# ScalarE instead of VectorE for one of two PSUM copies in the transposes of a retention + FFN kernel

## Chip, cores and metric

The kernel runs on one core of one Trainium2 chip. The metric is the device time of one execution in microseconds, lower is better. Four executions of the kernel before took 983.06, 985.38, 981.36 and 984.71 us, a median of 983.89 us.

The engines are called by the names that the profile uses: PE (matrix products, with PEld for its weight loads), DVE (VectorE), ACT (ScalarE), POOL (GpSimd) and SP (SyncE, which here only issues DMAs).

## What is computed

Attention with decay ("retention", without softmax) for 8 batches, 8 heads, 576 tokens and head dimension 64. Its output is laid out as 4608 tokens of 512 features, and goes through an FFN with a squared ReLU (512 to 2048 to 512). All of it is float32.

```python
scores = scale * np.matmul(q, k.transpose(0, 1, 3, 2))
gamma = 1.0 - 2.0 ** (-5.0 - np.arange(H, dtype=np.float32))
rel = pos[:, None] - pos[None, :]
Dmat = np.where(rel >= 0, gamma[:, None, None] ** rel[None, :, :], 0.0)
attn_out = np.matmul(scores * Dmat[None, :, :, :], v)
x = np.ascontiguousarray(attn_out.transpose(0, 2, 1, 3)).reshape(B * S, H * D)
h = np.maximum(x @ w_in, 0.0)
out = h * h @ w_out
```

## The kernel before

**Chunks.** The tokens of each batch are cut into chunks of 128, the last of a batch having 64: five chunks for each batch, 40 in all, numbered through. Chunks 4 and 9 are therefore short ones. A state per head (`u_ps` in PSUM, `u_sb` in SBUF) carries what earlier chunks of the batch leave to later ones. The finished tokens go to `xT` in SBUF, and blocks of 512 of them to the FFN.

**Order.** The program is written out in one order by hand, and each engine runs its own instructions in that order. The main loop (L753) runs over the chunks. For chunk numbers from 5 on, its body puts these calls one after the other:

- `retain_a(i - 1)` (L476): half of chunk i-1's own products into `x_ps`, and growth of the state, which ACT copies (L474);
- `turn(i)` (L414) while i is under `N_TURN` = 11, the function of the change;
- `ffn(i - 1, 0)` (L706): some steps of the FFN, enough to keep a pace;
- `retain_b(i - 1)` (L491): products of the earlier state with q (PE L500), and then L503, a tiny ACT copy of 128x2 that reads `x_ps` and writes into a state buffer;
- `scores(i)` (L428): k times q into PSUM (PE L443, 32 matmuls of 64x64, or 16 for a short chunk), masked by DVE (L451) and written over k's place;
- `retain_c(i - 1)` (L505): the other half of the chunk's own products (PE L465). The first of them waits for L503. Then ACT copies the result to `xT` (L522) and the state (L474);
- `ffn(i - 1, 1)`, and the loads of q, k and v for a later chunk.

Chunks 0 to 4 (`N_EARLY` = 4) have an order of their own at L754 to L795; chunk 4 is turned there, ahead of `retain_b(3)`.

**Turning q and k.** The products need q and k with the head dimension on the partitions. For chunks 0 to 10 PE transposes them through the identity matrix (L422): first k, then q, 64x64 at a time, into one PSUM tile `t_ps` of two banks. k and q of the first 64 tokens lie in the one bank, those of the second 64 in the other. Two copies bring them to the SBUF tile `qk`: k by ACT (L425), q by DVE (L426). From chunk 11 on, `flip` does without PE and PSUM: DVE transposes 32x32 blocks (L396) and ACT moves each to its place (L411, 416 copies of 32x256).

`t_ps` has one buffer (L107), and for chunks from 4 on `scores` takes the same one (L436). So PE can only start chunk i's scores when q and k of that chunk have been copied out, and can only turn the next chunk when DVE has masked the scores.

**What else these engines do in this stretch.** While chunks 4 to 10 are turned, FFN block 0 runs (`first_in`, L576: PE L586, ReLU by ACT at L591, squares by DVE at L594). Its weights come in as 64-bit floats and are turned to float32 in the meantime, 16 pieces of w_in, each by five DVE instructions (L210, L214, L222, L225, L228) with two ACT instructions (L218, L219) between the second and the third. POOL scales q (L376) and v (L453) when they have landed. SP issues all loads and stores of this stretch, in program order. From chunk 10 on, FFN blocks 1 and later run in a form with seven products (`ffn_in`, L607: PE L622, ACT L632 and L638, DVE L629 to L648). After the last chunk, a second long phase multiplies by w_out (PE L928).

Of the kernel before, what the change touches and what calls it, by code (L numbers as in the profile page):

```python
# [40 lines left out]
def kernel(  # L41
# [33 lines left out]
    nc = tc.nc  # L75
# [54 lines left out]
    N_EARLY = TOK // C  # L130
# [227 lines left out]
    def rows(half, n=64):  # L358
        return slice(64 * half, 64 * half + n)
# [24 lines left out]
    def new_qk(i):  # L384
        t = work3.tile([128, 2, HP, C], F32, tag="qk", name="qk")
        st[i]["qT"], st[i]["kT"] = t[:, 0, :, :], t[:, 1, :, :]
        return t
# [26 lines left out]
    def turn(i):  # L414

        cs = chunks[i][3]
        n_h = cs // CH
        p = ps_t.tile([128, 2, 512], F32, tag="t", name="t_ps").rearrange("p h (j d t) -> p h j d t", j=2, d=HP)
        for j in (1, 0):
            for hp in range(HP):  # L420
                for h in range(n_h):
                    nc.tensor.transpose(p[:, h, j, hp, :], loaded[i][j][rows(h), 2 * hp:2 * hp + 2, :],  # L422
                                        ident[rows(h), rows(h)])
        to = new_qk(i)[:, :, :, :cs].rearrange("p j d (h t) -> p j d h t", h=n_h)
        nc.scalar.copy(to[:, 1].rearrange("p d h t -> p h d t"), p[:, :n_h, 1, :, :])  # L425
        nc.vector.tensor_copy(to[:, 0].rearrange("p d h t -> p h d t"), p[:, :n_h, 0, :, :])  # L426

    def scores(i):  # L428

# [320 lines left out]
    warm(6, True)  # L750
    scale_q(0, nc.vector)
    turn(0)
    for i in range(N_CH + 1):  # L753
        if i <= N_EARLY:  # L754
# [5 lines left out]
            if i >= 1:  # L760
                retain_a(i - 1)
                if i < 3:
                    warm(4, False)
                elif i == N_EARLY:
                    turn(i)
                else:
                    convert(1)
                    first_in(1, (0,))
                    convert(5)
                retain_b(i - 1)  # L770
                if i < 3:
                    warm(4, False)
                retain_c(i - 1)
# [17 lines left out]
            if i < N_EARLY:  # L791
                if i < 2:
                    warm(6, False)
                if i + 1 < N_EARLY:
                    turn(i + 1)  # L795
# [283 lines left out]
```

## Time and profile before

The profiled execution took 983.06 us, of which 981.3 us are the span from the first to the last instruction. The table gives the busy time of each engine, in microseconds, in stretches of that span.

| stretch (us) | length | PE | PEld | DVE | ACT | POOL |
|---|---|---|---|---|---|---|
| 0 to 36 (start, chunks 0 to 3) | 36 | 28.57 | 24.87 | 19.33 | 13.64 | 13.04 |
| 36 to 102 (chunks 4 to 9 turned, FFN block 0) | 66 | 64.48 | 36.10 | 57.14 | 31.56 | 12.80 |
| 102 to 128 (chunk 10 turned, flips begin) | 26 | 24.54 | 19.09 | 20.82 | 13.84 | 5.59 |
| 140 to 155 | 15 | 14.81 | 12.34 | 14.83 | 9.01 | 3.97 |
| 155 to 400 | 245 | 237.01 | 201.19 | 206.79 | 154.98 | 58.17 |
| 400 to 981 (end of the first phase, w_out) | 581 | 574.68 | 548.49 | 453.50 | 107.04 | 30.09 |

PE's granted clock was 1.00 in all of these stretches but the first (0.95).

A busy share says how long an engine had something in hand, and not that its work set the pace. The table is only a first look; what an engine waited for, and for how long, is read from the views of waits and from the timeline.

### The profile page before, as it was taken

What the parts mean: (1) busy time and instruction counts of PE and PEld (TensorE: products, weight loads), DVE (VectorE), ACT (ScalarE), POOL (GpSimd) and SP (SyncE); (2) the same over time, 40 slices, a digit from 0 to 9 for tenths busy, and PEclk for the clock granted to TensorE, in tenths of its full rate; (3) what the DMA queues carried; (4) which work ended last, traced back from release to release, by engine and by line L of the source; (5) the groups of instructions that cost most, each with busy time, mean ns of one, the idle gap of its engine ahead of it and who ended that gap; (6) DMA issues with size and microseconds to landing.
All of it is one profiled execution on the core that took longest, in us unless ns stands there. A gap on an engine that the chain in (4) does not pass through costs nothing. (4 is left out here: it accounts for less than half of the span.)

```text
span 981.3 us, 24018 instructions
## 1 busy us (share of the span) xinstructions
PE 956.1 (97%) x10108; PEld 852.4 (87%) x10108; DVE 783.5 (80%) x1447; ACT 341.4 (35%) x848; POOL 127.4 (13%) x121
## 2 busy tenths in 40 slices
PE   7999999999999989989999999999999999999998
PEld 6745787888778878878888889999999999999998
DVE  3889799978887988788756588878888787887876
ACT  2554484674755855846541010000000000000000
POOL 3211223312122221213201000000000000000000
PEclk9999999999999999999999999999999999999999
DMA  9975656685586767656635966645353454534241
GB/s 201 246 222 150 179 154 161 213 274 147 153 240 197 208 173 235 172 144 140 236 135 232 361 246 247 226 161 184 108 204 116 175 186 174 204 116 172 87 172 43
DMA packets 172011, 181.43 MB, mean 185 GB/s; under 512 B 118144, under 2 KB 132480, under 8 KB 165248
## 3 DMA queue, kind: packets, MB, share of 16 engines
q1 hardware_dynamic: 169792, 179.38, 57.8%
q8 instruction: 79, 1.29, 0.5%
q10 hardware_dynamic: 2112, 0.52, 0.3%
q14 instruction: 28, 0.23, 0.1%
HBM read 109.36 MB, written 70.52 MB: 183 GB/s over the span
## 5 line engine op out<-in xcount | busy, mean ns | idle before, releaser
L622 PE MATMUL h_b<-room,w 128*128 128x256 f32 x768 | 186.6, 386 | 6.7 <-DVE room L641 3.7
L411 ACT COPY qk<-flip 32x256 f32<-32x256 f32 x416 | 167.4, 402 | 16.4 <-DVE flip L396 10.8
L622 PEld LDWEIGHTS h_b<-room,w 128*128 128x128 f32 x768 | 144.0, 191 | 29.0 <-DVE room L641 4.9
L928 PE MATMUL o_b<-w,room 128*128 128x128 f32 x1168 | 144.4, 275 | 0.2 <-DVE room L880 0.2
L928 PEld LDWEIGHTS o_b<-w,room 128*128 128x128 f32 x1168 | 137.2, 192 | 0.4 <-DVE room L880 0.4
L928 PE MATMUL o_c<-w,room 128*128 128x128 f32 x1008 | 123.0, 275 | 0.0
L622 PE MATMUL h_a<-room,w 128*128 128x256 f32 x512 | 122.5, 382 | 0.0
L622 PE MATMUL h_c<-room,w 128*128 128x256 f32 x512 | 122.1, 381 | 0.0
L928 PEld LDWEIGHTS o_c<-w,room 128*128 128x128 f32 x1008 | 117.7, 192 | 0.0
L942 ACT COPY r<-o_a 128x128 f32<-128x128 f32 x53 | 14.1, 266 | 271.7 <-PE o_a L928 236.1
L622 PEld LDWEIGHTS h_a<-room,w 128*128 128x128 f32 x512 | 96.0, 190 | 13.9 <-issue 0.5
L622 PEld LDWEIGHTS h_c<-room,w 128*128 128x128 f32 x512 | 96.4, 190 | 13.4
L928 PE MATMUL o_a<-w,a 128*128 128x128 f32 x688 | 85.6, 275 | 0.0
L928 PEld LDWEIGHTS o_a<-w,a 128*128 128x128 f32 x688 | 81.2, 192 | 0.1
L639 POOL TENSOR_TENSOR room<-room 128x512 f32<-128x512 f32 x32 | 34.8, 1088 | 346.2 <-ACT room L638 291.6
L629 DVE SCALAR_TENSOR_TENSOR room<-room 128x512 f32<-128x512 f32 x96 | 71.7, 747 | 3.3
L586 PE MATMUL h_ps<-room,w 128*128 128x512 f32 (+1 forms) x152 | 59.7, 540 | 1.4 <-DVE w L228 0.7
L465 PEld LDWEIGHTS x_ps<-qk,v_ld 64*64 64x64 f32 x1152 | 40.8, 138 | 19.5 <-issue 12.8
L641 DVE TENSOR_TENSOR room<-h_b,room 128x512 f32<-128x512 f32 x32 | 22.0, 687 | 44.6 <-PE h_b L622 44.6
L376 POOL TENSOR_TENSOR q_ld<-q_ld,dv 128x512 f32<-128x512 f32 (+1 forms) x39 | 45.0, 1153 | 92.8 <-DMA q_ld<-in_q_dram 72.0
L465 PE MATMUL x_ps<-qk,v_ld 64*64 64x64 f32 x1152 | 50.3, 227 | 6.4 <-ACT u_sb L503 6.0
L453 POOL TENSOR_TENSOR v_ld<-v_ld,dv 128x512 f32<-128x512 f32 (+1 forms) x40 | 48.5, 1214 | 12.9 <-DMA v_ld<-in_v_dram 12.9
(104 smaller groups left out, 1344.5 us busy)
## 6 DMA issues: line engine op xcount, KB each, us to landing
g_dram<-room SPq DMA_DIRECT2D x32, 1280.0 KB, 5.7
a<-g_dram SPq DMA_DIRECT2D x30, 1024.0 KB, 6.0
room<-g_dram SPq DMA_DIRECT2D x15, 1024.0 KB, 5.5
w<-w_dram SPq DMA_DIRECT2D x7, 1792.0 KB, 9.7
out_dram<-room SPq DMA_DIRECT2D x17, 512.0 KB, 3.3
w<-in_moe_w_in_dram SPq DMA_DIRECT2D x16, 512.0 KB, 5.5
w<-in_moe_w_out_dram SPq DMA_DIRECT2D x16, 512.0 KB, 3.8
v_ld<-in_v_dram SPq DMA_DIRECT2D x31, 256.0 KB, 3.6
```

The costliest lines, as they stand in the source:

```text
L376: engine.tensor_tensor(t, t, dv[:cs, :, NCH + ci:NCH + ci + 1].to_broadcast([cs, H, D]), op=ALU.mult)
L411: nc.scalar.copy(*moves.pop(0)[2:])
L453: nc.gpsimd.tensor_tensor(vs[:cs], vs[:cs], dv[:cs, :, ci:ci + 1].to_broadcast([cs, H, D]), op=ALU.mult)
L465: own.append(lambda hp=hp, e=e, b=b: nc.tensor.matmul(x_at(hp, b, h), lhsT=s["vs"][rows(h), 2 * hp + b, :], rhs=s["ret"][rows(h), e, hp, : ...
L586: nc.tensor.matmul(p.rearrange("p h t -> p (h t)"), lhsT=w[:, c, :], rhs=xT[0][:, c, lo * HT:hi * HT], start=(c == 0), stop=(c == N_DM - 1))
L622: nc.tensor.matmul(p[:, mm, :], lhsT=w[:, c, :], rhs=xs[n][right][:, c, :], start=(j in OPENS and mm == 0 and c == 0), stop=(j in CLOSES a ...
L629: nc.vector.scalar_tensor_tensor(t, t, 0.0, t, op0=ALU.max, op1=ALU.mult)
L639: nc.gpsimd.tensor_tensor(g["A11"], g["A11"], g["A11"], op=ALU.mult)
L641: nc.vector.tensor_tensor(g["A22"], p, p15, op=ALU.add)
L928: nc.tensor.matmul(p, lhsT=s["lefts"][left][:, m, :], rhs=w_out[j][:, m, WO_SLOT[right], :], start=(i in OPENS and m == 0), stop=(i in CLO ...
L942: nc.scalar.copy(r[:, 0, 0:128], p)
```

## The change

In `turn`, the copy of q is issued to DVE for chunks 0 to 3 as before, and to ACT for chunks 4 to 10. The copy has the same operands.

```diff
         nc.scalar.copy(to[:, 1].rearrange("p d h t -> p h d t"), p[:, :n_h, 1, :, :])
-        nc.vector.tensor_copy(to[:, 0].rearrange("p d h t -> p h d t"), p[:, :n_h, 0, :, :])
+
+        (nc.vector.tensor_copy if i < N_EARLY else nc.scalar.copy)(to[:, 0].rearrange("p d h t -> p h d t"), p[:, :n_h, 0, :, :])
```

Each of the seven moved copies stands directly behind the copy of k in ACT's order. Everything else keeps its place on every engine. The waits that the framework puts in change with it:

- the first matmul of `scores` (L443) waits for ACT, and for PE's own transposes, where it waited for DVE;
- ten FFN matmuls (eight of L586, two of L622) now carry a wait for DVE of their own, which the wait at L443 had covered before;
- three of DVE's maskings (L451) and two of its squares (L594) carry a wait for ACT that the copy of q had carried for them.

## Prediction

> **What bounds the kernel now.** I read the shares first. The first two lines of the page:
>
> ```profile
> span 981.3 us, 24018 instructions
> ...
> PE 956.1 (97%) x10108; PEld 852.4 (87%) x10108; DVE 783.5 (80%) x1447; ACT 341.4 (35%) x848; POOL 127.4 (13%) x121
> ```
>
> PE leaves 25 us of the span idle, 7.4 of them before 36 us. Work taken from DVE is worth only what PE waits for it. So the second view is PE's waits while chunks 4 to 10 are turned (36 to 114 us), and the third the line of the moved copy in the same stretch:
>
> ```profile
> engine line waited for: us in total, times, longest us
> PE h_ps L586 <- ACT room L522: 0.7, 1, 0.7
> PE sc_ps L443 <- DVE qk L426: 0.6, 2, 0.4
> PE x_ps L465 <- ACT u_sb L503: 0.3, 1, 0.3
> ```
>
> ```profile
> L426 DVE COPY qk<-t_ps x7: 416/683/691, 38.4 to 112.7; 128x512 f32<-128x512 f32 x5, 128x256 f32<-128x256 f32 x2
> its engine sat idle before it (us, times) until:
> who waited for it (us, times):
>   PEld sc_ps L443: 0.8, 2
>   PE sc_ps L443: 0.6, 2
> ```
>
> The reader is to see that PE waited in two of the seven chunks, and that DVE never sat idle ahead of the copy: it came late because DVE's queue was full. Fourth, the timeline, sorted here by start time, around the worst of the two, chunk 5:
>
> ```profile
> 44.15 0.58 ACT L425 COPY qk<-t_ps 128x512 f32<-128x512 f32 x1
> 44.63 0.73 ACT L218 ACTIVATE w<-w,exp_bias 128x512 uint32<-128x512 uint32 x1
> 45.25 0.69 ACT L219 ACTIVATE w<-w 128x512 f32<-128x512 uint32 x1
> 45.96 0.46 PE L500 MATMUL x_ps<-qk,u_sb 64*64 64x64 f32 x16
> 46.06 0.68 DVE L426 COPY qk<-t_ps 128x512 f32<-128x512 f32 x1
> 46.06 0.38 ACT L591 ACTIVATE room<-h_ps 128x256 f32<-128x256 f32 x1
> 46.48 0.16 ACT L503 COPY u_sb<-x_ps 128x2 f32<-128x2 f32 x1
> 46.79 0.69 PE L443 MATMUL sc_ps<-qk 64*64 64x64 f32 x32 [0.38 <-DVE qk L426]
> 47.31 0.64 PE L465 MATMUL x_ps<-qk,v_ld 64*64 64x64 f32 x16
> ```
>
> k was out of PSUM at 44.73 us; q was copied from 46.06 to 46.74, and L443 started 0.05 us later.
>
> **What is removed, PE by issue times.** PE's idle figure understates such a wait, because modelled ends overlap the next start; starts are better. With nothing to wait for, L443 starts 0.28 us after an L500 of 16 matmuls (59.84 to 60.12, chunk 6) and 0.52 us after one of 32 (100.92 to 101.44, chunk 9). By chunk: 4, no L500 directly ahead and no wait; 5, 46.79 - 45.96 = 0.83, so 0.55 lost; 6, none; 7, 73.24 to 74.12 = 0.88, so 0.36 lost; 8, 87.17 to 87.87 = 0.70, so 0.18 lost (DVE's copy ended at 87.81, and the waits view has no entry); 9, none; 10, 113.91 to 114.19 = 0.28, none. Upper bound of the direct gain: 0.55 + 0.36 + 0.18 = 1.09 us.
>
> **What is added.** Seven ACT copies, of the very shape and source of L425: five of 0.59 us and two of 0.37. In a busy row the next instruction starts earlier: 0.48 us after a 128x512 copy (44.15 to 44.63), 0.25 after a 128x256 (56.72 to 56.97, L474). So ACT's queue grows by 5 x 0.48 + 2 x 0.25 = 2.9 us, DVE's shrinks by 5 x 0.60 (46.06 to 46.66) + 2 x 0.34 = 3.7 us.
>
> ACT's delay matters where PE waits behind it, and that is L503, for which L465 waits. Chunk by chunk: chunk 4, ACT idle 0.28 us ahead of L503, the copy needs 0.25: nothing. Chunk 6, 1.19 idle ahead of L591: hidden. Chunk 7, L218 moves from 71.11 to 71.35, and 0.95 idle ahead of the next L591 takes it. Chunk 8, 1.18 idle; chunk 9, 3.26; chunk 10, 1.33: hidden. Only chunk 5 has no gap: 44.15 + 0.48 = 44.63 for q, L218 at 45.11, L219 0.62 later at 45.73, L591 0.59 after that (43.26 to 43.85 elsewhere) at 46.32, L503 at 46.74. A waiting L465 starts 0.22 us after L503 starts (127.31 to 127.53), so 46.96 instead of 47.31. Chunk 5 gains 0.35, not 0.55. In chunk 7, L503 at 74.00 lets L465 start at 74.22, and L443 with its 0.52 of issue at 73.24 + 0.52 + 0.52 = 74.28 against 74.64: the whole 0.36. In chunk 8, 0.18 likewise. Sum: 0.35 + 0.36 + 0.18 = 0.89 us.
>
> Two other queues stand behind ACT. DVE's L222 waits for L219: in chunk 5 it next needs it at 46.7 us and has it at 46.4; later it waits for an L219 that is released by PE's L586 (2.00 us at 66.81), so DVE's saved time turns into longer waiting there. PE needs a converted piece of weights 4.7 us or more after its L228 (sixth piece ready 49.46, used at 56.21; the tenth 70.11, used at 75.21), so half a microsecond either way is nothing. SP's stores and weight loads that wait for DVE (L594, L228), with the loads of q, k, v behind them, move with PE or earlier.
>
> New waits: ten on FFN matmuls, six L443 with two conditions instead of one. All their conditions are long met. An L622 group with a met DVE wait starts 1.73 us after the group ahead (121.94 to 123.67), one without 1.83 (115.42 to 117.25): no price seen. The upper end is a semaphore instruction of 0.017 us (two in ACT's queue at L503): 16 x 0.017 = 0.27. I take 0, nearest to the matmul rows.
>
> [...]
>
> **What comes after.** PE's gain has to survive the stalls that follow:
>
> ```profile
> 119.49 0.27 PE L465 MATMUL x_ps<-qk,v_ld 64*64 64x64 f32 x2 [0.34 <-POOL v_ld L453]
> 127.53 0.27 PE L465 MATMUL x_ps<-qk,v_ld 64*64 64x64 f32 x2 [1.11 <-ACT u_sb L503]
> 159.07 0.27 PE L465 MATMUL x_ps<-qk,v_ld 64*64 64x64 f32 x2 [1.47 <-ACT u_sb L503]
> ```
>
> Followed back, these go to PE: POOL at 118.38 stands behind an L376 released by loads that SP issued after a store of the L594 at 106.93, in turn after PE's L586; ACT's full row to 127.31 starts at an L474 that PE released at 120.25; DVE's full row ahead of 159 starts at an L641 that waited 0.63 us for PE. If all links keep their length, everything shifts by 0.89. Sum: 983.06 - 0.89 = 982.2 for the profiled execution. That execution is 0.83 below the median of the runs shown (983.89), so against the median I expect 983.0. Something within 0.3% (2.95 us) cannot be told from no change with this kernel, whose runs spread over 4.0 us.
>
> **Rivals.**
> *Absorbed.* Load landings set by DMA traffic and not by PE hold the 119.49 wait in place; it grows from 0.34 to 1.2 us and takes the gain. For it: POOL's L376 at 116.36 waited 15.16 us for a load. Against: that load's issue follows PE. Time 983.9. Chance 0.20.
> *More than shifted.* The relief on DVE and the new phase also clear later stalls: 0.34 + 1.11 + 0.19 (151.06, DVE L641) + 1.47 = 3.1 us more. For it: DVE was busy 14.83 of 15 us from 140 to 155. Against: from 102 to 117 DVE idles four times (1.83, 1.56, 0.91, 1.85 us), so nothing it saved earlier is still there. Time 983.9 - 4.0 = 979.9. Chance 0.15.
> *Slower: POOL falls on other DVE work.* While POOL scales q and v, DVE instructions beside it take 1.43 to 1.56 us instead of 0.69 (L240 at 98.75, L562 at 124.25, L241 at 135.45, L228 at 148.85). POOL's start hangs on landings; a new phase may put it on four more instructions in the full DVE rows ahead of the stalls at 151 to 159 us: 4 x 0.86 = 3.4. Time 983.0 + 3.4 = 986.4. It decides from the second such instruction on (1.7 against a gain of 0.9). Against: POOL's number of instructions is unchanged, and some overlaps will go as others come. Chance 0.15.
>
> **How the numbers follow.** The shift has a chance of 0.50. Its own range: a gain from 0 to 1.1, less 0.27 for the waits, and about 1 us for the spread of medians: 981.8 to 985.1. The whole range goes to the faster rival, 980.0, and up to a slower one of three overlaps, 983.0 + 2.6 = 985.6, widened to 985.9 for the waits. Faster by over 0.3% (under 980.9) is most of the third case: 0.14. Slower by over 0.3% (above 986.8) is the part of the fourth where more than four overlaps come, with room for a queue that I have followed wrongly: 0.12. Within: 0.74.
>
> **What would show it.** L443 starts 0.28 us (chunk 5) and 0.52 us (7, 8) after L500, with no wait for a copy of q; L465 of chunk 5 waits for L503. ACT has 14 copies for chunks 4 to 10, each q 0.48 us after its k; DVE's waits for L219 are longer by what it saved. PE's start of chunk 10's L500 is at 113.0 instead of 113.91. The prediction is wrong if that start moved by 0.9 and the end did not, or if PE waits for L503 in chunks 6 to 10, or if the stalls from 119 to 159 us change by more than 1 us in sum.

## The result and the profile after

The changed kernel has a median of 982.77 us (53 executions, 978.38 to 986.38). The kernel before, run beside it, has 984.16 us (79 executions). The ratio is 0.9981, with a 95% interval of 0.9974 to 0.9988: a gain of 1.85 us, between 1.2 and 2.6. That lies within the 0.3% named in the prediction, and inside its range, but it is twice the forecast 0.89.

The profiled execution of the changed kernel took 981.62 us. The top of its page:

```profile
span 979.5 us, 24027 instructions
...
PE 955.0 (97%) x10108; PEld 852.4 (87%) x10108; DVE 777.3 (79%) x1440; ACT 344.4 (35%) x855; POOL 128.3 (13%) x121
```

Seven instructions went from DVE to ACT, and PE has as much to do as before. PE's waits from 36 to 114 us, and the line of the copy of q in the same stretch:

```profile
engine line waited for: us in total, times, longest us
PE h_ps L587 <- ACT room L523: 0.7, 1, 0.7
PE x_ps L466 <- ACT u_sb L504: 0.3, 1, 0.3
```

```profile
L427 ACT COPY qk<-t_ps x7: 378/593/615, 37.7 to 112.3; 128x512 f32<-128x512 f32 x5, 128x256 f32<-128x256 f32 x2
its engine sat idle before it (us, times) until:
who waited for it (us, times):
```

(The lines below L425 are one higher than before: L443 is now L444, L500 L501, L503 L504.) The two other waits are the old ones, the wait for q is gone, and the copy neither waited nor was waited for. The timeline of chunk 5, first ACT and then PE:

```profile
44.89 0.57 ACT L425 COPY qk<-t_ps 128x512 f32<-128x512 f32 x1
45.35 0.59 ACT L427 COPY qk<-t_ps 128x512 f32<-128x512 f32 x1
45.83 0.73 ACT L218 ACTIVATE w<-w,exp_bias 128x512 uint32<-128x512 uint32 x1
46.45 0.70 ACT L219 ACTIVATE w<-w 128x512 f32<-128x512 uint32 x1
47.04 0.37 ACT L592 ACTIVATE room<-h_ps 128x256 f32<-128x256 f32 x1
47.30 0.15 ACT L504 COPY u_sb<-x_ps 128x2 f32<-128x2 f32 x1
```

```profile
46.66 0.46 PE L501 MATMUL x_ps<-qk,u_sb 64*64 64x64 f32 x16
46.94 0.65 PE L444 MATMUL sc_ps<-qk 64*64 64x64 f32 x32
47.51 0.68 PE L466 MATMUL x_ps<-qk,v_ld 64*64 64x64 f32 x16
```

q is out of PSUM at 45.94 us, a full microsecond before L444 needs it. L444 starts 0.28 us after L501, which is the issue time that the prediction used.

The two profiled executions can be laid side by side by the start of the first L500 of a chunk (L501 after). As in the prediction, "chunk 5's L500" is the one ahead of the scores of chunk 5, in the same pass of the loop (by `retain_b(i - 1)` it works for chunk 4). Chunk 5: 45.96 before, 46.66 after. So the changed kernel came 0.70 us later out of the first 36 us. Chunk 10: 113.91 and 113.59, so it gained 1.02 in between. Chunk 24: 311.70 and 311.62, 0.24 lost again. Chunk 33: 432.17 and 430.44, a further 1.65 gained, far behind the last changed instruction. A dip of PE's granted clock that only the execution before had stands there (0.50 from 429 to 432 us; below). One pair of profiles thus mixes the change with differences between executions that are as large as the change itself. That is why nearly all that follows is read by chunk.

### The profile page after: what moved, and what is told of

It reads as the page before. It is cut to its first block, busy times and chain, and to the rows that moved or that the text cites. A ratio compares the mean times of both kernels' runs of the same rounds, so it can differ in the third digit from the quotient of the medians.

```text
span 979.5 us, 24027 instructions
## 1 busy us (share of the span) xinstructions
PE 955.0 (97%) x10108; PEld 852.4 (87%) x10108; DVE 777.3 (79%) x1440; ACT 344.4 (35%) x855; POOL 128.3 (13%) x121
## 5 line engine op out<-in xcount | busy, mean ns | idle before, releaser
L623 PEld LDWEIGHTS h_a<-room,w 128*128 128x128 f32 x512 | 96.0, 190 | 13.9 <-issue 0.5
L466 PEld LDWEIGHTS x_ps<-qk,v_ld 64*64 64x64 f32 x1152 | 40.8, 138 | 19.6 <-issue 12.8
L466 PE MATMUL x_ps<-qk,v_ld 64*64 64x64 f32 x1152 | 50.4, 228 | 6.5 <-ACT u_sb L504 6.0
```

What stands on the lines that cost most here:

```text
L466: own.append(lambda hp=hp, e=e, b=b: nc.tensor.matmul(x_at(hp, b, h), lhsT=s["vs"][rows(h), 2 * hp + b, :], rhs=s["ret"][rows(h), e, hp, : ...
L623: nc.tensor.matmul(p[:, mm, :], lhsT=w[:, c, :], rhs=xs[n][right][:, c, :], start=(j in OPENS and mm == 0 and c == 0), stop=(j in CLOSES a ...
```

## The experiments

The runs are called e1 to e12, by the order of their labels. Two theories stood at the start. A: the change is worth what the prediction counted, about 1 us, and the rest of the measured gain is chance. B: there is a second part of about 0.9 us that one profile doesn't show. The yardstick is the time from a chunk's first L500 to the next chunk's, since PE is busy for 97% of the span. Executions differ in their start phase, and this takes it out.

**The same two kernels again** (no edit), five rounds each on one chip.

> The kernel before, unchanged, against itself. Theory A (the change is worth the 1.0 us that PE gains from 36 to 102 us, and the rest of the measured 1.85 us is chance in where the granted clock dips): ratio 1.000, its interval within 0.9985 to 1.0015; executions whose mean granted clock is 1.000 have spans 1.0 us longer than such executions of the changed kernel (median 977.2 there, so about 978.2). Theory B (the change also takes away about 0.9 us somewhere that one profile does not show): such executions have spans about 979 us.

> The changed kernel once more, beside the kernel before. Theory A: ratio 0.9990 (1.0 us); PE's first L501 of chunks 5, 6, 8, 9 keeps its distances: 13.42 us from chunk 5's to chunk 6's (13.88 before), 26.97 from chunk 6's to chunk 8's (27.33), 13.56 from chunk 8's to chunk 9's (13.75). Theory B: ratio 0.9981 again, with the same distances.

The kernel before against itself: ratio 1.001 (0.9995 to 1.0025). The changed kernel: 982.12 us, ratio 0.997 (0.9955 to 0.9986). So the gain is there again, and the interval leaves out A's 1.0 us (0.9990) again, as the first did, both narrowly. The other sign, the spans of executions whose mean granted clock is 1.000, could not be read: the kernel before had none. What the page of a second execution of the kernel before shows is the finding of this study. Chunk 5 there, DVE and then PE:

```profile
43.19 0.43 DVE L210 TENSOR_SCALAR w<-w 128x512 uint32<-128x512 uint32 x1 [0.74 <-DMA w<-in_moe_w_in_dram]
...
45.31 0.69 DVE L228 SCALAR_TENSOR_TENSOR w<-w,w 128x512 uint32<-128x512 uint32 x1
45.92 0.68 DVE L426 COPY qk<-t_ps 128x512 f32<-128x512 f32 x1
```

```profile
45.13 0.46 PE L500 MATMUL x_ps<-qk,u_sb 64*64 64x64 f32 x16
46.66 0.69 PE L443 MATMUL sc_ps<-qk 64*64 64x64 f32 x32 [1.07 <-DVE qk L426]
```

DVE's row of conversions, with the copy of q at its end, stood 0.74 us waiting for a load of weights. PE then waited 1.07 us for q, where the profile of the prediction had 0.38 and no wait of L210 at all. The same place in the changed kernel's second execution:

```profile
43.44 0.43 DVE L210 TENSOR_SCALAR w<-w 128x512 uint32<-128x512 uint32 x1 [1.43 <-DMA w<-in_moe_w_in_dram]
```

```profile
44.62 0.46 PE L501 MATMUL x_ps<-qk,u_sb 64*64 64x64 f32 x16
44.90 0.65 PE L444 MATMUL sc_ps<-qk 64*64 64x64 f32 x32
```

The load makes DVE wait twice as long, and PE loses nothing: L444 starts 0.28 us after L501.

**Only some of the chunks.** In the kernel before, the copy of q goes to ACT in chunk 5 alone, in 7 and 8 alone, or in the other four alone:

```diff
-        nc.vector.tensor_copy(to[:, 0].rearrange("p d h t -> p h d t"), p[:, :n_h, 0, :, :])
+        (nc.scalar.copy if i == 5 else nc.vector.tensor_copy)(to[:, 0].rearrange("p d h t -> p h d t"), p[:, :n_h, 0, :, :])
```

In the other two the condition is `i in (7, 8)` and `i in (4, 6, 9, 10)`.

> q of chunk 5 alone by ACT. Theory (each chunk's gain is PE's own wait there, and they add up): from PE's first L500 of chunk 5 to that of chunk 6 13.42 us as in the changed kernel, from chunk 6's to chunk 8's 27.33 and from chunk 8's to chunk 9's 13.75 as before. Rival (what counts is DVE's lighter queue as a whole): 13.88 or little less in the first, and a share of the gain in each of the later ones.

> q of chunks 7 and 8 alone by ACT. Theory: chunk 5's L500 to chunk 6's 13.88 us as before, chunk 6's to chunk 8's 26.97, chunk 8's to chunk 9's 13.56, both as in the changed kernel. Rival (lighter DVE queue as a whole): the two gains are smaller, since chunks 4, 5 and 6 leave DVE as full as before.

> q of chunks 4, 6, 9 and 10 alone by ACT; 5, 7 and 8 stay with DVE. Theory (only PE's own waits for the copy count): PE's first L500 of chunk 5 to chunk 6's 13.9 to 14.6 us, chunk 6's to chunk 8's 27.3 to 27.9, chunk 8's to chunk 9's 13.75, all as in the two profiles of the kernel before (13.88 and 14.58, 27.33 and 27.82, 13.75 and 13.74). Rival (DVE's lighter queue as a whole): clearly less, towards 13.42, 26.97 and 13.56.

Distances of PE's L500 in us, with those of the runs above; bold where ACT copies q:

| run | chunk 5 to 6 | 6 to 7 | 7 to 8 | 8 to 9 |
|---|---|---|---|---|
| before, profile of the prediction | 13.88 | 13.40 | 13.93 | 13.75 |
| before again (e1) | 14.58 | 13.40 | 14.42 | 13.74 |
| only 4, 6, 9, 10 (e5) | 16.58 | **13.40** | 14.35 | 13.64 |
| only 7, 8 (e4) | 13.90 | 13.39 | **13.57** | **13.56** |
| only 5 (e3) | **13.41** | 13.50 | 14.46 | 13.63 |
| after | **13.42** | **13.40** | **13.57** | **13.56** |
| after again (e2) | **13.53** | **13.40** | **13.57** | **13.56** |

Each chunk gets its gain from its own copy, and chunks 4, 6, 9 and 10 give nothing, as predicted (4 to 5 took 9.37 or 9.38 us and 9 to 10 12.98 or 12.99 in every one of these runs). The 16.58 of e5 lies outside the 13.9 to 14.6 that was expected; what it holds is seen in the last run below. With q by ACT the distances hardly vary. With q by DVE they vary by up to 2.7 us from execution to execution, and the profile of the prediction happened to be at the short end in chunks 5 and 7. The times of these single executions are 981.45, 983.62 and 987.82 us. They are of no use to the question, since a dip of the clock elsewhere can move any one of them by 1.65 (the one at 428 us in the profile of before).

**Is it q's earliness or DVE's relief?** In the changed kernel, DVE gets a multiplication of the size of the copy, in the copy's old place; its result is not used.

```diff
+            w = 256 * n_h
+            ones = idle[:, 0:1].to_broadcast([128, w])
+            nc.vector.tensor_tensor(W[6][:, 3072:3072 + w], ones, ones, op=ALU.mult)
```

> The changed kernel with a DVE multiplication of the same size, of data that nobody needs, put where the copy of q stood: DVE's queue is as long as before, q comes early from ACT. Theory (the gain is that q comes early): 13.42, 26.97 and 13.56 us as in the changed kernel. Rival (the gain is DVE's relief): 13.9 or more, 27.3 or more, 13.75.

DVE's row was as full as before the change, and L210 in chunk 5 waited 1.57 us for its load. Distances: 13.66, 13.40, 13.56, 13.56. The gain stayed, but for 0.2 us in chunk 5, where L471 (the L465 of before) waited 0.17 us for ACT. So the gain is that q comes out of PSUM without standing in DVE's queue; what DVE saves shows no worth in these distances but for that 0.2.

**Is ACT's slack as counted?** In the changed kernel, ACT copies q twice:

```diff
+            nc.scalar.copy(to[:, 0].rearrange("p d h t -> p h d t"), p[:, :n_h, 0, :, :])
             nc.scalar.copy(to[:, 0].rearrange("p d h t -> p h d t"), p[:, :n_h, 0, :, :])
```

> The changed kernel with q of chunks 4 to 10 copied twice by ACT: its queue grows by another 2.9 us. Prediction's account of ACT's slack: only chunk 5 has none; its L504 comes 0.48 us later, and chunk 5 to 6 takes 13.9 us instead of 13.42; chunk 6 to 8 stays at 26.97 to 27.05 and chunk 8 to 9 at 13.56. Rival (ACT had no slack to give): each short segment grows by about 0.48 us, 1.4 us in sum.

Chunk 5 grew from 13.42 to 14.02, and chunks 7 and 8 stayed at 13.57 and 13.55. The timeline of chunk 5, ACT and then PE:

```profile
43.34 0.60 ACT L429 COPY qk<-t_ps 128x512 f32<-128x512 f32 x1
43.98 0.58 ACT L430 COPY qk<-t_ps 128x512 f32<-128x512 f32 x1
...
45.92 0.14 ACT L507 COPY u_sb<-x_ps 128x2 f32<-128x2 f32 x1
```

```profile
44.95 0.65 PE L447 MATMUL sc_ps<-qk 64*64 64x64 f32 x32
46.11 0.68 PE L469 MATMUL x_ps<-qk,v_ld 64*64 64x64 f32 x16 [0.51 <-ACT u_sb L507]
```

Only chunk 5 has no gap in ACT's row. There the second copy reaches PE through the tiny copy (L503 of before), as the prediction had laid it out; in the others ACT's idle time takes it.

**All eleven chunks.** In the kernel before, ACT copies q in chunks 0 to 3 too:

```diff
-        nc.vector.tensor_copy(to[:, 0].rearrange("p d h t -> p h d t"), p[:, :n_h, 0, :, :])
+        (nc.scalar.copy if i >= 0 else nc.vector.tensor_copy)(to[:, 0].rearrange("p d h t -> p h d t"), p[:, :n_h, 0, :, :])
```

> q of all turned chunks by ACT, 0 to 3 too, where DVE's copy waited 4.9 us for ACT's copy of k. Theory (PE waits there only for the first chunk, 1.40 us, of which the hand-over is about 0.25): 0.25 us less than the changed kernel, not to be told from it: ratio 0.998. [...] Rival: ACT is late with the state copies of the first chunks, 0.5 us more each: ratio 0.9995 or above.

982.57 us, ratio 0.9981 (0.9965 to 0.9998), the same as the changed kernel. The 4.9 us by which the first q copies had waited for k's copy (DVE idle 1.41, 2.10 and 1.43 us ahead of L426 in chunks 0 to 2 of the profile of before) are not to be had: PE's waits for q in the first 36 us only changed their releaser (L443 for ACT's copy, 1.2 us there, where it was 1.4 for DVE's). No version here is shown to beat the changed kernel.

**DVE's queue made longer.** In the kernel before, the same multiplication stands directly ahead of DVE's copy of q, from chunk 4 on:

```diff
+        if i >= N_EARLY:
+            w = 256 * n_h
+            ones = idle[:, 0:1].to_broadcast([128, w])
+            nc.vector.tensor_tensor(W[6][:, 3072:3072 + w], ones, ones, op=ALU.mult)
         nc.vector.tensor_copy(to[:, 0].rearrange("p d h t -> p h d t"), p[:, :n_h, 0, :, :])
```

> The kernel before with a DVE multiplication of 0.60 us, of data that nobody needs, directly ahead of each copy of q for chunks 4 to 10. Theory (PE waits for a copy that stands in DVE's queue, so whatever is ahead of it there is paid by PE once the slack is gone): chunk 5 to 6 14.5 us or more (13.88 to 14.58 in the kernel before, 16.58 in one profile with a clock dip), chunk 6 to 8 27.9 or more, of which chunk 7 to 8 14.5 to 15.0, chunk 8 to 9 14.35 (13.75), chunk 6 to 7 13.5 (13.40, slack of 0.47 used up). Rival (DVE's lateness there is set by PE and takes such an addition up): as before. The changed kernel took the same addition without loss in chunks 7 and 8 (13.56 each) and at most 0.24 in chunk 5.

```profile
PE sc_ps L447 <- DVE qk L430: 2.4, 3, 1.0
```

That line of PE's waits (36 to 114 us) stands against 0.6 in two times before. L210 of chunk 5 had no wait in this execution, and 13.88 became 14.49: the whole 0.60 us of the added instruction (45.64 to 46.24 in DVE's row) reached PE. Chunk 7 had 14.70, chunk 8 14.22, and chunk 6, which had some room, 13.51. So what stood ahead of the copy in DVE's queue was paid by PE, in chunk 5 in full and in chunk 6 by 0.11 us. With the copy on ACT and DVE kept as busy (e6), it pays no more than the 0.2 us of chunk 5.

**POOL beside DVE.** Two extra POOL multiplications, meant to lie beside DVE's row ahead of chunk 7's copy, in the kernel before and in the changed one:

```diff
+        if i == 6:
+            ones = idle[:, 0:1].to_broadcast([128, 512])
+            for _ in range(2):
+                nc.gpsimd.tensor_tensor(W[6][:, 3072:3584], ones, ones, op=ALU.mult)
```

> The kernel before with two more POOL multiplications of 128x512 behind the scaling of v of chunk 6, of data that nobody needs, so that POOL is busy some 2 us longer while DVE converts weights ahead of chunk 7's copy of q. Theory (DVE instructions beside POOL's take up to 1.5 us in place of 0.69, and that is what makes chunk 7's copy late): two or three more such instructions, chunk 7 to 8 14.9 to 16.0 us instead of 13.93 to 14.46. Rival (chunk 7's wait has another cause): 13.9 to 14.5.

> The same two POOL multiplications in the changed kernel. Theory: chunk 7 to 8 stays at 13.57 us, since PE waits there for ACT alone. Rival: as much longer as in the kernel before.

The aim missed: POOL ran them at 52.5 to 55.9 us, ahead of chunk 6's copy. Chunk 7 to 8 took 14.36 us in the kernel before, inside the rival's 13.9 to 14.5, and 13.57 in the changed one; with nothing added there, neither decides about chunk 7. For chunk 6 they do say something. In the kernel before, DVE:

```profile
51.56 1.28 DVE L214 TENSOR_SCALAR w<-w 128x512 uint32<-128x512 uint32 x1
53.15 1.14 DVE L222 SCALAR_TENSOR_TENSOR w<-w,w 128x512 f32<-128x512 uint32 x1 [0.30 <-ACT w L219]
54.32 1.41 DVE L225 TENSOR_TENSOR w<-w,w 128x512 f32<-128x512 f32 x1
```

and PE:

```profile
60.44 0.69 PE L443 MATMUL sc_ps<-qk 64*64 64x64 f32 x32 [0.42 <-DVE qk L426]
```

DVE's instructions beside POOL took 1.1 to 1.4 us instead of 0.42 and 0.69, and a chunk that never waits otherwise waited: 13.94 us from chunk 6 to 7 instead of 13.40. In the changed kernel with the same POOL work the distance is 13.53. What is left there comes by way of ACT: L218 waited 0.87 us for L210, which came late in DVE's slowed row, the tiny copy started at 58.55, and the first matmul behind it at 58.75, 0.67 us after L444 where it is 0.53 in the changed kernel.

**The kernel before a third time** (no edit, one execution), to see how far its chunks 5 and 7 vary.

> The kernel before, one more profile, for the size of its waits from one execution to the next. Theory (the profile shown before the change was a lucky one): chunk 5 to 6 between 13.88 and 14.9 us, according to whether DVE's L210 had to wait for a weight load; chunk 7 to 8 between 13.93 and 14.5; chunk 8 to 9 13.64 to 13.75. Rival (that profile was typical, and the others were off): 13.88, 13.93, 13.75 within 0.05.

Chunk 5 to 6 took 16.61 us, outside the expected 13.88 to 14.9; 7 to 8 took 14.30. The wait in chunk 5 was 1.39 us, and something else came with it. PE's busy time and granted clock (the third number from the right), microsecond by microsecond:

```profile
45.00:46.00 1.00, 0.27 (x16) 0.13 (x10) 0.97 (x3) 0.46 (x2) 0.00 (x0) 1.00 1.09 369
46.00:47.00 1.00, 0.34 (x21) 0.34 (x24) 1.00 (x4) 0.00 (x0) 0.00 (x0) 1.00 1.10 353
47.00:48.00 1.00, 1.00 (x42) 0.93 (x34) 0.96 (x3) 0.13 (x1) 0.00 (x0) 0.93 1.20 306
48.00:49.00 1.00, 1.00 (x2) 0.49 (x2) 0.97 (x2) 0.24 (x1) 0.00 (x0) 0.50 1.17 234
49.00:50.00 1.00, 1.00 (x2) 0.36 (x2) 1.00 (x3) 0.00 (x0) 0.00 (x0) 0.50 0.86 171
50.00:51.00 1.00, 1.00 (x2) 0.34 (x1) 1.00 (x4) 0.00 (x0) 0.23 (x1) 0.50 0.46 94
51.00:52.00 1.00, 1.00 (x3) 0.39 (x2) 1.00 (x1) 0.00 (x0) 1.00 (x2) 0.87 1.07 239
```

PE's clock fell to half for 3.4 us. From L443 to the next chunk's L500 it took 14.75 us (46.66 to 61.41), where the second execution took 13.05 (46.66 to 59.71): 1.70 us more. The run with only chunks 4, 6, 9 and 10 had the same wait (1.38) and the same dip. With the waits of 0.38 to 1.07 us the clock stayed at 1.00.

## Why the prediction was right, and why too small

Chunk 5 in all runs but e7 and e9, in which the queue that holds the copy of q was made longer: with DVE's copy and then with ACT's, each ordered by L210's wait. "Room" is from L500 to L443.

| run | q by | L210 starts (its wait for the load) | L500 | L443 | room |
|---|---|---|---|---|---|
| before | DVE | 43.20 (0) | 45.96 | 46.79 | 0.83 |
| only 7, 8 (e4) | DVE | 42.35 (0) | 45.08 | 45.93 | 0.85 |
| before, more POOL (e10) | DVE | 43.04 (0.39) | 45.33 | 46.51 | 1.18 |
| before again (e1) | DVE | 43.19 (0.74) | 45.13 | 46.66 | 1.53 |
| only 4, 6, 9, 10 (e5) | DVE | 43.12 (0.98) | 44.76 | 46.59 | 1.83 |
| before, third (e12) | DVE | 43.19 (1.07) | 44.80 | 46.66 | 1.86 |
| after | ACT | 43.97 (0) | 46.66 | 46.94 | 0.28 |
| all by ACT (e8) | ACT | 44.87 (0) | 47.56 | 47.85 | 0.29 |
| after, more POOL (e11) | ACT | 42.18 (0.41) | 44.38 | 44.66 | 0.28 |
| only 5 (e3) | ACT | 43.36 (1.39) | 44.65 | 44.93 | 0.28 |
| after again (e2) | ACT | 43.44 (1.43) | 44.62 | 44.90 | 0.28 |
| DVE kept busy (e6) | ACT | 44.01 (1.57) | 45.06 | 45.34 | 0.28 |

With DVE's copy, L443 starts 3.47 us after L210 when L210 had to wait, and 3.58 or 3.59 when it hadn't. Where L210 waits, the chunk starts when the load allows it and not when PE is there. An execution whose first 36 us went well then gains nothing from that: PE comes early to chunk 5 and waits longer. The profile of the prediction was one of the two in which L210 had no wait. That PE came latest there, at 45.96, did not decide it: in e4 it came at 45.08, and the room was nearly as short (0.85), since the load was in. With ACT's copy the room is 0.28 or 0.29 whatever the load does.

Point by point, by the prediction's own steps:

- **What is removed.** This is the step that was mis-sized: "Upper bound of the direct gain: 0.55 + 0.36 + 0.18 = 1.09 us" was read from one profile and was no upper bound. Over the five executions in which chunk 5 was as before (before, e1, e4, e5, e12) its distance averages 15.11 us, against 13.47 in the two of the changed kernel: 1.64. Over the five with chunk 7 as before (before, e1, e3, e5, e12) 14.29 against 13.57: 0.72. Chunk 8: 13.68 against 13.56, 0.12. The sum is 2.5 us. With e10 as a sixth execution for chunk 5 (14.23; its added work lies behind that chunk's scores) the mean there is 14.96, and the sum 2.3. The mean span of all executions for which it is on record differs by 2.33 (982.65 of 54 before, 980.32 of 66 changed, which were for the most part not run together).
- **Why q was late.** "It came late because DVE's queue was full" holds, but the prediction took the queue's length as fixed. Two things lengthen it: L210's wait for a load of weights (chunk 5, in four of six executions), and the instructions that DVE runs beside POOL (chunk 7). The second was known to the prediction, as a rival that makes the changed kernel slower. In every profile of this study two instructions of DVE lie beside POOL ahead of chunk 7's copy, and their length varies; the one shown had 1.11 and 1.43 us. Here are e1's, with POOL's and the consequences:

```profile
66.68 1.60 DVE L222 SCALAR_TENSOR_TENSOR w<-w,w 128x512 f32<-128x512 uint32 x1 [2.00 <-ACT w L219]
68.31 1.43 DVE L225 TENSOR_TENSOR w<-w,w 128x512 f32<-128x512 f32 x1
...
73.73 0.68 DVE L426 COPY qk<-t_ps 128x512 f32<-128x512 f32 x1
```

```profile
66.67 1.06 POOL L376 TENSOR_TENSOR q_ld<-q_ld,dv 128x512 f32<-128x512 f32 x1 [13.62 <-DMA q_ld<-in_q_dram]
67.68 1.50 POOL L453 TENSOR_TENSOR v_ld<-v_ld,dv 128x512 f32<-128x512 f32 x1
```

```profile
74.47 0.69 PE L443 MATMUL sc_ps<-qk 64*64 64x64 f32 x32 [0.67 <-DVE qk L426]
```

  The 0.49 us by which L222 is longer than in the profile of before are the 0.49 by which the distance is (14.42 to 13.93). In the changed kernel the same two took 0.83 and 1.43, and no matmul waited. For chunk 7 that is read from rows that vary by themselves; the run that made POOL's row longer (e10) shows the same path in chunk 6.
- **The clock.** No step of the prediction had it. In two of the six executions with chunk 5 as before (e5, e12) the wait, 1.38 and 1.39 us and the longest of the six, was followed by PE's clock at half, for another 1.70 us. With these two segments at 14.9 instead, the mean gain of chunk 5 over the five named above is 0.96 and not 1.64. How often it happens can't be told from six.
- **What is added.** ACT's pitches held (0.46 to 0.48 us per copy of 128x512). In chunk 5, L503 was to lie 0.42 us behind the ReLU (46.32 to 46.74); it lies 0.26 behind (47.04 to 47.30). The prediction had read the 0.42 off the profile before (46.06 to 46.48), where L500 ended only at 46.42; in ACT's full row the distance is shorter. L504 is hardly late any more: L466 follows L444 by 0.57 us, where L465 followed L443 by 0.52, and the wait for L503 that the prediction named as a sign is not among PE's waits (with DVE kept busy, e6, it was 0.17). So chunk 5 gained 0.46 (13.88 to 13.42) against the profile shown, and not 0.35; chunk 7's 0.36 and chunk 8's 0.19 were as predicted. For that one profile the sum was 1.01 and not 0.89, a small error beside the one above. Chunk 10's L501 came at 113.59 and not at the 113.0 that was named, because this execution was 0.70 late out of the first 36 us.
- **New waits, taken as nothing.** L444 starts 0.28 us (chunk 5) and 0.52 us (7 and 8: 73.48 to 74.00, 87.05 to 87.57) after L501, the issue times exactly.
- **DVE's copy behind ACT's.** In chunks 0 to 2 in the profile of before, DVE started the copy of q 0.03 us after ACT's copy of k had ended, and had stood idle for 4.9 us in sum. Ahead of the seven moved copies it had no idle time, and no gain is seen from ending such waits: with q by ACT in all eleven chunks (e8) the ratio is 0.9981, and 0.9981 and 0.997 in the two measurements of the changed kernel.
- **What comes after.** The gain survived. PE's waits from 114 to 162 us after the change:

```profile
PE x_ps L466 <- ACT u_sb L504: 2.6, 2, 1.5
PE x_ps L466 <- POOL v_ld L454: 0.4, 1, 0.4
PE h_b L623 <- DVE room L642: 0.2, 1, 0.2
```

  Before, they were 2.6, 0.3 and 0.2. The absorbed rival would have needed 1.2 in the second line. "More than shifted" had the direction of the error right but the mechanism wrong: these stalls did not shrink. The slower rival did not come: with q on ACT, POOL's overlaps in this stretch don't reach PE, or reach it at a quarter (e11).
- **What lies around the span.** The prediction left it as it was. It grew from 1.73 us (1.67 to 1.79) to 2.08 (2.02 to 2.14) in all executions, which takes 0.35 back from 2.33 and leaves 1.98, beside the measured 1.85 (1.2 to 2.6). What it consists of the profile doesn't show. The partial versions have 1.6 to 1.8, so it doesn't go with the number of ACT's copies.

So theory A falls by the two intervals, and B holds: a part that the one profile doesn't show lies in chunk 5 (the wait for the load, and the clock behind it) and in chunk 7 (DVE beside POOL). That these parts are the whole of the difference is not shown, as the next paragraph says. The forecast's range held by its width; its 0.89 was half of what was measured.

**What stays open.** The load of weights lands in chunk 5 at 42.2 us or earlier, and up to 44.0; why was not tried. The mean span shows the sum of the parts, but the frequency of the dip at 48 us is unknown. Executions whose mean granted clock is 1.000, without any dip, came 9 times in 66 with the changed kernel (and 3 in 12 with all by ACT) and never in 54 before. The dip at 48 us explains a part of that, but the profiles before, e1 and e4 were without it there and still had dips elsewhere. From 100 us to the last microseconds, before had one dip, e1 and e12 had two each, and the two profiles of the changed kernel none. The mean granted clock is 0.9947 in the 54 executions and 0.9959 in the 66, which is worth some 1.2 us of the span (an estimate, 0.0012 of 980; dips of the first 36 us are in it too), where two dips of 1.70 in six would give 0.6. Whether the change makes later dips rarer or these executions happened to have fewer was not tried, and if it is a part of the gain, the agreement of 2.5 with 2.33 is partly luck. In four of the profiles with q on ACT (after, e2, e6, e11), PE loses 0.2 to 0.4 us around 305 us (chunk 23 to 24 took 13.19 to 13.38 us instead of 12.98), and nothing read in the profiles says for what; e7 and e8 do not lose it.

## What to carry to other kernels

A wait read in one profile is one draw. Before its length is used as the price, look at what stands ahead of the late instruction in its engine's queue: if that includes an instruction that waits for a DMA (here L210, 0 to 1.07 us in six profiles), or one whose duration another engine stretches (here L222, 1.11 to 1.60 us in before, e1, e9 and e12), the wait can vary from execution to execution (PE's in chunk 5 from 0.38 to 1.39 us), and a second profile of the unchanged kernel is worth more than a closer reading of the first. An instruction that the busiest engine needs goes to a queue in which nothing ahead of it waits for memory, if there is one with room (here L443 started 0.28 or 0.29 us after L500 with ACT's copy, and 0.83 to 1.86 with DVE's). And a stall of PE can cost more than its length: two waits of 1.4 us here were each followed by another 1.70 us, in clock.

## What the hardware showed that was not expected

**After a wait of 1.4 us PE's clock was at half for 3.4 us.** It cost 1.70 us both times (e5 and e12 in chunk 5). Longer waits elsewhere had such a dip behind them in some executions only. The execution of the kernel before that the prediction used, at 428 us:

```profile
428.60 3.64 PE L622 MATMUL h_b<-room,w 128*128 128x256 f32 x8 [1.99 <-DVE room L641]
```

The third execution had a wait of the same length in the same work:

```profile
433.75 1.99 PE L622 MATMUL h_b<-room,w 128*128 128x256 f32 x8 [1.98 <-DVE room L641]
```

The eight matmuls took 3.64 us in the one and 1.99 in the other, after 1.99 and 1.98 us of waiting. Such dips, which cost 1.65 to 1.7 us, came around 255, 295 and 430 us, in a different choice of places in each execution (255 and 295 in e10, 430 in the one that the prediction used). Each moves an execution by about as much as the whole change does. Three of these dips, read from the granted clock, were equally long: 3.4 us at half in chunk 5 of e5 and of e12, and 3.4 us at 429 us in the execution before. The two in chunk 5 came behind waits of 1.38 and 1.39 us, with PE busy 0.6 of the two microseconds from 45 to 47. What starts a dip is not shown, nor that the wait alone brought them on.

**DVE beside POOL.** DVE's elementwise instructions of 128x512 took 0.8 to 1.6 us instead of 0.69 (L222 ahead of chunk 7: 0.83 after, 1.60 in e1), and up to 1.28 instead of 0.42 (L214 in e10), when a POOL instruction ran beside them. How much of an instruction's time is covered varies from execution to execution, and so does its length (the same L222: 0.83 after, 1.11 before, 1.27 in e4 and 1.60 in e1).
